# Routed attention and a gated feed-forward layer: mask products in tiles of 32 rows, and the work of three engines placed anew

## The chip, the cores and the metric

The kernel runs on one core of a Trainium2 chip. A core has TensorE (matrix products into PSUM), VectorE, ScalarE and GpSimd (work on whole tiles), and queues of DMAs, here mostly SyncE's. [...]semaphores tie the engines together. The metric is the device time of one execution in microseconds (us).

In the lines of the profile PE is TensorE, PEld its weight loads, DVE VectorE, ACT ScalarE, POOL GpSimd, SPq SyncE's DMA queue. A product's shape, such as 64*128, is rows by columns of the array that it uses. Every operation is recorded through one helper (line 63), so the tiles' names tell the groups apart.

## What is computed

```python
B, H, S, D = 4, 8, 768, 64 ; n_clusters = 16        # q, k, v: (B, H, S, D)
q_assign = argmax(einsum('bhsd,hcd->bhsc', q_n, c_n))   # q_n, k_n, c_n: unit length
k_assign = argmax(einsum('bhsd,hcd->bhsc', k_n, c_n))
mask = q_assign[:, :, :, None] == k_assign[:, :, None, :]
scores = where(mask, q @ k.T / sqrt(D), -1e9)
scores = scores - max(scores, axis=-1)
attn = exp(scores) ; attn = attn / (sum(attn, axis=-1) + 1e-9)
x = (attn @ v) as (B*S, H*D) = (3072, 512)
h = x @ w_in                                        # (3072, 2048)
out = (h * erf(softplus(h))) @ w_out                # (3072, 512)
```

All in float32 from outside. A query sees only the keys that fall to the same one of 16 centroids.

## The kernel before

**Two stages.** First the attention, for 16 pairs of heads (p = 0 to 15). Then the feed-forward layer in chunks of 512 tokens, its products by a scheme with seven products in place of eight, which needs sums of blocks ("forms", `left_forms` and `right_forms`, lines 518 and 527).

**A pair.** The two heads e = 0 and 1 of a pair lie on partitions 0 to 63 and 64 to 127 of transposed tiles qT and kT, so a product over D = 64 uses half of the array's rows, and those of the two heads go beside each other. A unit of work is 128 keys (j = 0 to 5) by one half of the queries (384), for both heads; a pair has 12 units. A *period* (`period(p, i)`, i = 0 to 5) handles two of them.

**What the mask is made of.** `choose` (VectorE: sims, the largest, hot, hotT) gives each token a one-hot row over the 16 centroids. `masks` multiplies it by the constant `pick` (64 rows) into PSUM, and ScalarE copies it to qm (0 or 1) or km (0 or -BIG, by `scale` and `bias=nbig`). qm and km have 64 rows a head: 16 for the centroids, and one (row SH = 32) that carries a shift in qm and 1 in km. The product km x qm added to q x k then gives the score less a shift where the centroids agree, and something hugely negative elsewhere.

**The shift** is a bound on the largest score, found one half ahead, by `maxima_step`: for 128 queries (t) and a half of the keys, TensorE multiplies bf16 copies qv, kv (call it v) and then adds qm x km (m) on the same PSUM tile `wide`; VectorE reduces the 768 columns to a maximum. Two steps make a period. After six of them a small reduce writes `lowest`, six products turn it (`turn`), and two copies (ScalarE, 1x384) put it into row SH of qm, before the scores of that half.

**Order of TensorE in a period**: turn (i = 0 and 3), v1 m1, `products` of both units (q x k, float32, into the two PSUM tiles sc), v2 m2, `scores` of both units (km x qm added: s and s'), similarities of the pair after the next (i = 3), `attend` of the two units before (128 keys by 64 columns), and at i = 0 and 3 the divide's products with `minus`. The four mask products of a pair stand in `MASKS` by period and place: place 0 ahead of `products`, 1 behind them, 2 behind the scores.

**The other engines.** ScalarE: exp of the two sc tiles (`curve`, into pr), the mask copies, the copies qv and kv, two steps (Ln, Exp) of the divide. VectorE: the reduces, transposes of the loaded q and k, `choose`, the rest of the divide. GpSimd: sums of pr over the keys (`accumulate`, into a part of more_out). All three also turn the feed-forward weights, loaded as 64-bit words, into float32, in small steps spread over the periods: `size_and_rest` and `sign` (ScalarE), `bounded` and `shifted` (VectorE), `summed` (GpSimd), for two of 22 pieces in a pair. The table `FORMS` says in which periods of pairs 11 to 15 VectorE computes the forms of w_in and of the first x.

**Order.** Most engines' instructions stay as the program writes them (`InOrder`). Later DMAs are issued on SyncE's queue where the framework places them. Buffers that matter: `wide` is single, sc double, pr eight deep, `turned[0]` and `turned[1]` are two PSUM banks which take turns for attend, divide, turn, similarities and the mask products.

Of the kernel before, what the change touches and what calls it, by code (L numbers as in the profile page):

```python
# [36 lines left out]

UP = 2.0**16
PLACES = 5
FORMS = {  # L40
    11: {5: 1}, 12: {0: 1, 2: 1, 5: 1}, 13: {0: 1, 2: 1, 5: 1}, 14: {0: 2, 2: 1, 3: 1, 5: 1},
    15: {0: 1, 2: 1, 3: 2, 4: 2, 5: 2},
}
BIG = 2.0**60
FLOOR = 2.0**50
EPS = 2.0**-70
SH = 2 * C
NPT = NJ + 2
N_LATE = 10
LAST_X = 11  # L50
MASKS = {(0, 1): ("k", 0), (2, 0): ("q", 0), (2, 2): ("k", 1), (5, 0): ("q", 1)}
FIRST_MASKS = {(2, 0): ("k", 0), (2, 1): ("q", 0), (2, 2): ("k", 1), (5, 0): ("q", 1)}


class InOrder:
# [16 lines left out]
def kernel(  # L72
# [157 lines left out]
    def fetch(n):  # L230
# [2 lines left out]
        words = t.rearrange("p (n w) -> p n w", w=2)  # L233
        steps[n] = words[:, :, 1], words[:, :, 0], t.bitcast(I16)[:, 1 : 4 * LC : 4]

    def size_and_rest(n):
        w, (hi, lo, _) = w_steps[n][0], steps[n]
        ae.activation(out=w, in_=hi, func=ACT.Abs, scale=UP)
        ae.activation(out=lo.bitcast(I32), in_=lo.bitcast(U32), func=ACT.Copy, scale=2.0**-29)

    def bounded(n):
        w = w_steps[n][0]
# [15 lines left out]

    ve.memset(nbig, 0.0)
    for e in range(2):  # L260
        ve.memset(nbig[e * D : e * D + C], -BIG)
        ve.memset(nbig[e * D + SH : e * D + SH + 1], 1.0)
    for t in maxima:
        ve.memset(t, FLOOR)
    ve.memset(pick, 0.0)
# [81 lines left out]
        if p < NPAIR:  # L347
            ae.copy(out=pairs[p][nm + "v"], in_=pairs[p][nm + "T"])

    def masks(p, nm, half, bank):  # L350

        if p >= NPAIR:
            return lambda: None
        st = pairs[p]
        cols = slice(half * HW, (half + 1) * HW)
        r = slice(0, D) if nm == "q" else slice(D, P)
        won = bank[:, 0:HW]
        te.matmul(won, lhsT=pick[r, half], rhs=st["hotT"][r], start=True, stop=True)
        if nm == "q":
            return lambda: ae.activation(out=st["qm"][:, cols], in_=won, func=ACT.Relu)  # L360
        return lambda: ae.activation(
            out=st["km"][:, cols], in_=won, func=ACT.Identity, bias=nbig, scale=BIG
        )

    turns = []

    def maxima_step(p, i, sm=wide):

        st = pairs[p]
        nmx = maxima[p % 2]  # L370
        t, half = divmod(i, 2)
        for a, b, start in (("qv", "kv", True), ("qm", "km", False)):
            for e in range(2):
                r = slice(e * D, (e + 1) * D)
                te.matmul(
                    sm[:, e, 0:HW], lhsT=st[a][r, t * P : (t + 1) * P],
                    rhs=st[b][r, half * HW : (half + 1) * HW], start=start, stop=not start,
                )
        ve.tensor_reduce(
            out=nmx[:, :, t, half], in_=sm[:, :, 0:HW], axis=AX.X, op=ALU.max, negate=True  # L380
        )
        if i in (NJ - 1, 2 * NJ - 1):
            h = i // NJ
            ve.tensor_reduce(
                out=lowest[h][:, :, SH::D].rearrange("p t e -> p e t"),
                in_=nmx[:, :, h * HJ : (h + 1) * HJ], axis=AX.X, op=ALU.min,
            )
            turns.append((p, h))

    def turn(p, h, copies=(ae.copy, ae.copy)):  # L390

        st = pairs[p]
        pn = turned[h][:, 0:HW].rearrange("p (t n) -> p t n", t=HJ)
        for t in range(HJ):
            for e in range(2):
                cols = slice(e * D, (e + 1) * D)
                te.matmul(pn[cols, t], lhsT=lowest[h][:, t, cols], rhs=identb, start=True, stop=True)
        for e, copy in zip(range(2), copies):
            r = slice(e * D + SH, e * D + SH + 1)
            copy(out=st["qm"][r, h * HW : (h + 1) * HW], in_=pn[r].rearrange("p t n -> p (t n)"))  # L400
        st["shift", h] = True

# [20 lines left out]
    def scores(u):  # L423

        p, half, j = units[u]
        st = pairs[p]
        sc = sc_of[u]
        assert ("shift", half) in st
        for e in range(2):
            r = slice(e * D, (e + 1) * D)  # L430
            te.matmul(
                sc[:, e, 0:HW], lhsT=st["km"][r, j * P : (j + 1) * P],
                rhs=st["qm"][r, half * HW : (half + 1) * HW], start=False, stop=True,
            )
# [226 lines left out]
        sums_of[n, s, lot] = gsp.tile([P, 3, FG, P], F32, name="g_more")  # L661
        return left_forms(ve, *g_parts(n, s, lot))

    def rest(n):
        return [lambda: None] * n

    def gates(n, lot, which=(0, 1), between=()):
        work = list(between)
        for s in which:
            curves, products_of = gate(n, lot, s)  # L670
            if s == which[0]:
                work = [curves] + work + rest(7 - len(work)) + products_of
            else:
                work += [curves, *sums, *rest(3)] + products_of
            sums = add_hidden(n, lot, s)
        return work + sums

# [27 lines left out]
    def run(work):  # L705
        for _ in work:
            pass

    def step_ahead(u):
        p, i = divmod(u + NJ, 2 * NJ)
        if p < NPAIR:
            maxima_step(p, i)

    forms = sum((left_forms(ve, *w_in_parts(f, 2)) for f in range(0, HF, 2)), [])
    routing = [iter(())]
    part = [iter(())]

    def period(p, i):  # L720
# [4 lines left out]
        def mask(place):  # L725
            which = (MASKS if p else FIRST_MASKS).get((i, place))
            if which:
                return masks(p + 1, *which, turned[0 if i in (0, 5) else 1])
            return lambda: None

        if u > 0:
# [3 lines left out]
            step_ahead(u)  # L735
        mask(0)()
        next(part[0], None)
        if u == 2:
            next(routing[0])
        products(u)  # L740
        products(u + 1)
        mask(1)()
        if u > 0:
            step_ahead(u + 1)
        next(part[0], None)
        scores(u)
        scores(u + 1)
        later = mask(2)
        if i == 3:
            similarities(p + 2)  # L750
            routing[0] = choose(p + 2)
        curve(u)
        later()
        curve(u + 1)
        if u == 0:
# [5 lines left out]
            vectors(1, "q")  # L761
            vectors(1, "k")
        if i == 0 and early(n1 - 1):
            shifted(n1 - 1)
            sign(n1 - 1)
        elif i == 1 and early(n1):
            size_and_rest(n1)
        elif i == 2 and early(n1):
            bounded(n1)
        elif i == 3 and early(n1):  # L770
            shifted(n1)
            sign(n1)
        elif i == 4 and early(n2):
            size_and_rest(n2)
        elif i == 5 and early(n2):
            bounded(n2)
        for work in forms[: FORMS.get(p, {}).get(i, 0)]:
            work()
            forms.remove(work)
        if i == 3:  # L780
            for _ in range(3):
                next(routing[0], None)
        if i == 0:
            if p:
                transposes(p + 2, "q")
        elif i == 1:
            load(p + 1, "v", v, vp)
            if p == 0:
                run(routing[0])
                transposes(2, "q")  # L790
        elif i == 2:
            transposes(p + 2, "k")
        elif i == 4:
            vectors(p + 2, "k")
        elif i == 5:
            run(routing[0])
            vectors(p + 2, "q")
        if u > 0:
            for w in (u - 2, u - 1):
                accumulate(w)  # L800
            if i == 1 and early(n1 - 1):
                summed(n1 - 1)
            elif i == 4 and early(n1):
                summed(n1)
            for w in (u - 2, u - 1):
                attend(w)
            if i % HJ == 0:
                part[0] = divide(u - 1)
                next(part[0])
        mask(3)()  # L810


# [23 lines left out]
    for r in (0, D):  # L836
        for half in range(2):
            for e in range(2):
                c = r + half * Q + e * C
                ve.tensor_copy(  # L840
                    out=pick[r : r + D, half, e * D : e * D + C], in_=first[r : r + D, c : c + C]
                )
    also = ps_s.tile([P, 2, 512], F32, name="sc", tag="s")
    products(0)
# [11 lines left out]
    for n in range(PLACES - 1):  # L856
        fetch(n)
    for i in range(NJ):
        maxima_step(0, i, also if i % 2 else wide)
        if i == 1:  # L860
            masks(0, "q", 1, turned[1])()
        if i < NJ - 1:
            warm(2, turned[0], zeros)
# [7 lines left out]
    for p in range(NPAIR):  # L871
# [3 lines left out]
            load_x(0)  # L875
            load_x(1)
        if p == LAST_X + 2:
            forms += right_forms(ve, *x_parts(0))
    for work in forms:
        work()  # L880
    u = len(units)
    for w in (u - 2, u - 1):
# [46 lines left out]
    aside_work += all_weights(0, 4) + out_forms[0] + out_forms[1]  # L929
    hidden(0, 0, {0: finish_attention})  # L930
    finish_aside()
    aside_work += together(rest(2) + gates(0, 0, (0,)), all_weights(4, N_LATE))
    hidden(0, 1, pace=2, first=ve.tensor_copy)
    finish_aside()
    for n in range(NCHUNK):
# [5 lines left out]
        project(n, 0, 2 if n else 3)  # L941
        finish_aside()
        if n == 0:
            aside_work += together(gates(0, 1, (1,)), rest(2) + [fence] + out_forms[2] + out_forms[3])
            hidden(1, 0, first=ve.tensor_copy)
        elif n + 1 < NCHUNK:
            hidden(n + 1, 0)
# [41 lines left out]
```

## Time and profile before

| | us |
|---|---|
| median of 3 runs | 1015.81 (1015.75 to 1015.94) |
| the profiled execution | 1015.54 |
| its span, first to last instruction | 1013.8 |
| attention: start to the last attend product | 0 to 429.4 |
| feed-forward layer | 429.3 to 1013.8 |
| one pair of heads in the steady part (p = 1 to 10) | 25.83 |
| mean granted TensorE clock | 1.000 |

The costliest operations of the attention, from the groups by shape (mean of one):

| engine, operation | count | ns |
|---|---|---|
| TensorE km,qm or kv,qv, 64*128, 384 columns bf16 | 756 | 322, 328 |
| TensorE q x k, 64*128, 384 columns float32 | 768 | 484, 482 |
| TensorE attend, 128*64, 386 columns float32 | 768 | 500 |
| VectorE reduce for the maxima | 189 | 956 |
| ScalarE exp | 192 | 810 |
| GpSimd add of pr | 160 | 1750, 1847 |
| VectorE transpose of 768 columns | 30 | 963 to 972 |
| ScalarE mask copies km, qm | 63 | 578, 494 |
| ScalarE size, rest, sign of a weight piece | | 679, 682, 1368 |
| VectorE bounded, shifted of a weight piece | | 417, 417 |

The length of one product [...]is longer than the distance between two starts. That is why distances of starts are used for TensorE.

### The profile page before, as it was taken

To read this page: it belongs to the slowest core of one execution; us is meant where nothing else is said; L and a number is where in the kernel's file an instruction comes from. 1 tells how busy PE (TensorE), PEld (TensorE's weight loads), DVE (VectorE), ACT (ScalarE), POOL (GpSimd) and SP (SyncE) were. 2 spreads that over 40 slices of the span, in tenths; PEclk is the share of its full clock that TensorE was granted. 3 is DMA by queue.
4 is the path that set the end of the run, shared out by engine and by line. 5 is a ranking of instruction groups with operands and counts; after the bars stand their busy time and mean duration, and the time that the engine had idled before them with its cause. 6 is when DMAs were issued, how large, how long until landed. Compare 5 with 4: busy or idle time off the path is not lost.

```text
span 1013.8 us, 15440 instructions
## 1 busy us (share of the span) xinstructions
PE 1006.4 (99%) x5930; PEld 724.0 (71%) x5930; DVE 695.5 (69%) x1305; ACT 513.5 (51%) x673; POOL 346.5 (34%) x229
## 2 busy tenths in 40 slices
PE   8999999999999999999999999999999999999998
PEld 3555555555555555488888888888888888888887
DVE  8777777777777777879766564756565647565753
ACT  3788888888887666467714232222324150505050
POOL 1777777777777667844030000000000000000000
PEclk9999999999999999999999999999999999999999
DMA  9344444444344311052000100110001000000001
GB/s 218 67 103 100 99 103 104 105 105 105 83 105 104 63 32 33 16 174 68 17 1 33 51 1 1 42 42 1 18 24 42 1 22 22 1 1 21 21 1 41
DMA packets 141641, 55.55 MB, mean 55 GB/s; under 512 B 127104, under 2 KB 131456, under 8 KB 141568
## 3 DMA queue, kind: packets, MB, share of 16 engines
q1 hardware_dynamic: 139216, 54.28, 20.9%
q8 instruction: 46, 0.75, 0.3%
q10 hardware_dynamic: 2352, 0.30, 0.2%
q14 instruction: 27, 0.22, 0.1%
HBM read 41.98 MB, written 12.58 MB: 54 GB/s over the span
## 4 chain that ended last, share of the span: by engine, by line
PE 97%; DVE 1%; DMA 1%; POOL 0%; ACT 0%; SPq 0%; issue 0%; DVEq 0%; ACTq 0%; POOLq 0%
PE bank L63 43%; PE turned L63 32%; PE sc L63 15%; PE wide L63 7%; DVE nmx L63 1%; POOL more_out L63 0%; DMA in_k<-in_k_dram 0%; DMA in_q<-in_q_dram 0%; DVE kT L63 0%; SPq L63 0%; DVE sims L63 0%; ACT inv L63 0%; DVE qT L63 0%; ACT pr L63 0%; DVE den L63 0%
## 5 line engine op out<-in xcount | busy, mean ns | idle before, releaser
L63 POOL TENSOR_TENSOR more_out<-more_out,pr 128x768 f32<-128x768 f32 x128 | 224.0, 1750 | 68.0 <-ACT pr L63 62.9
L63 DVE TENSOR_REDUCE nmx<-wide 128x2 f32<-128x768 f32 x189 | 180.7, 956 | 88.6 <-PE wide L63 64.3
L63 ACT ACTIVATE pr<-sc 128x768 f32<-128x768 f32 x192 | 147.1, 810 | 78.1 <-PE sc L63 78.1
L63 PE MATMUL turned<-pr,in_v 128*64 128x386 f32 x768 | 145.4, 500 | 0.1
L63 DVE TENSOR_TENSOR g<-bank,g 128x256 f32<-128x256 f32 x222 | 89.5, 421 | 53.2 <-PE bank L63 46.7
L63 PE MATMUL bank<-x_own,w_in 128*128 128x256 f32 x424 | 104.5, 380 | 0.0
L63 PE MATMUL bank<-w_out,g 128*128 128x256 f32 x448 | 103.1, 379 | 0.0
L63 PE MATMUL sc<-qT,kT 64*128 64x384 f32 x528 | 99.7, 484 | 0.0
L63 PEld LDWEIGHTS turned<-pr,in_v 128*64 128x64 f32 x768 | 46.6, 136 | 69.8 <-issue 65.1
L63 PEld LDWEIGHTS bank<-w_out,g 128*128 128x128 f32 x448 | 85.1, 190 | 11.6
L63 PEld LDWEIGHTS bank<-x_own,w_in 128*128 128x128 f32 x424 | 80.3, 190 | 12.2 <-issue 1.2
L63 ACT COPY g<-bank 128x256 f32<-128x256 f32 x28 | 10.4, 372 | 152.2 <-PE bank L63 148.2
L63 DVE TENSOR_TENSOR osb<-bank,osb 128x256 f32<-128x256 f32 x87 | 35.4, 419 | 72.8 <-ACT osb L63 25.4
L63 ACT ACT_TABLE_LOAD x48 | 61.6, 1283 | 45.9 <-DVE g L63 40.9
L63 POOL TENSOR_TENSOR more_out<-pr,pr 128x768 f32<-128x768 f32 x32 | 59.1, 1847 | 50.0 <-ACT pr L63 38.5
L63 PE MATMUL bank<-x_more,more_in 128*128 128x256 f32 x296 | 76.0, 379 | 0.0
L63 PEld LDWEIGHTS <-qv 64*128 64x128 bf16 x384 | 25.6, 93 | 65.2 <-issue 51.0
L63 PE MATMUL wide<-kv,qv 64*128 64x384 bf16 x378 | 69.4, 328 | 1.1 <-ACT km L63 0.6
L63 PE MATMUL wide<-km,qm 64*128 64x384 bf16 x378 | 68.3, 322 | 0.0
L63 PEld LDWEIGHTS sc<-qT,kT 64*128 64x128 f32 x528 | 56.2, 187 | 16.6 <-issue 1.2
L63 PE MATMUL bank<-more_out,g_more 128*128 128x256 f32 x272 | 64.3, 379 | 0.0
L63 DVE TENSOR_TENSOR g<-a_s,g 128x512 f32<-128x512 f32 x96 | 62.4, 687 | 1.4 <-ACT a_s L63 1.4
(162 smaller groups left out, 1704.8 us busy)
## 6 DMA issues: line engine op xcount, KB each, us to landing
x_own<-in_moe_w_in_dram SPq DMA_DIRECT2D x13, 512.0 KB, 4.0
in_v<-in_v_dram SPq DMA_DIRECT2D x32, 192.0 KB, 2.9
x_dram<-more_out SPq DMA_DIRECT2D x32, 192.0 KB, 2.2
x_own<-x_dram SPq DMA_DIRECT2D x6, 1024.0 KB, 5.1
out_dram<-osb SPq DMA_DIRECT2D x23, 256.0 KB, 2.0
in_k<-in_k_dram SPq DMA_DIRECT2D x59, 96.0 KB, 2.6
in_q<-in_q_dram SPq DMA_DIRECT2D x58, 96.0 KB, 3.1
g_more<-in_moe_w_out_dram SPq DMA_DIRECT2D x6, 512.0 KB, 3.4
```

Of the source, the lines that this page charges most:

```text
L63: ins = getattr(self.engine, name)(*args, **kw)
```

## The change

- Within the 64 rows a head, qm and km are laid out anew. The shift's row is now row 0; the centroids stand in rows 1 to 16, and once more in rows 33 to 48. `pick` writes both copies. In km the second copy has 0 in its own shift row. So rows 0 to 31 alone make a mask with shift, and rows 32 to 63 alone a mask without.
- `scores` multiplies only rows 0 to 31 of each head. The second maxima step of a period takes its mask passes (m2) from rows 32 to 63, and they are issued behind the first `scores`. v2, m1 and the passes of other steps keep 64 rows. TensorE's order is v1 m1, products, v2, s, m2, s'.
- Mask products of place 2 use 32 rows (`narrow`); k's first half moves from place 1 of period 0 to place 2 there, q's second half from place 0 of period 5 to place 2. The copy of km for k's first half is VectorE's.
- Work of VectorE and ScalarE stands in other periods: hotT in period 0 between the two reduces, the q transpose in period 5 (of the pair three ahead), both bf16 copies in period 4, `bounded` and `shifted` in periods 0 and 3, `size` at the end of period 3 and `rest` in period 5. `choose` puts its maxima beside an sc tile, not beside `wide`. GpSimd takes `summed` ahead of its adds.
- Of the 20 forms, up to eight are GpSimd's, two in each of pairs 12 to 15; VectorE's stand in pairs 12 to 15.
- The remaining lines rename `rest` to `idle` and add memsets for `nbig`.

```diff
-FORMS = {
-    11: {5: 1}, 12: {0: 1, 2: 1, 5: 1}, 13: {0: 1, 2: 1, 5: 1}, 14: {0: 2, 2: 1, 3: 1, 5: 1},
-    15: {0: 1, 2: 1, 3: 2, 4: 2, 5: 2},
-}
+FORMS = {12: {0: 1}, 13: {0: 1}, 14: {0: 1, 3: 1}, 15: {0: 1, 3: 2, 4: 2, 5: 2}}
+POOL_FORMS = range(12, 16)
-SH = 2 * C
-MASKS = {(0, 1): ("k", 0), (2, 0): ("q", 0), (2, 2): ("k", 1), (5, 0): ("q", 1)}
+MASKS = {(0, 2): ("k", 0), (2, 0): ("q", 0), (2, 2): ("k", 1), (5, 2): ("q", 1)}
...
-        ve.memset(nbig[e * D : e * D + C], -BIG)
-        ve.memset(nbig[e * D + SH : e * D + SH + 1], 1.0)
+        for n in range(2):
+            r = e * D + n * Q
+            ve.memset(nbig[r : r + C + 1], -BIG)
+            ve.memset(nbig[r : r + 1], 1.0 - n)
...
-    def masks(p, nm, half, bank):
+    def masks(p, nm, half, bank, narrow=False, copied_by=ae):
...
+        if narrow:
+            r = slice(r.start + half * Q, r.start + (half + 1) * Q)
         won = bank[:, 0:HW]
         te.matmul(won, lhsT=pick[r, half], rhs=st["hotT"][r], start=True, stop=True)
...
+        if copied_by is ve:
+            return lambda: ve.tensor_scalar(
+                out=st["km"][:, cols], in0=won, scalar1=BIG, scalar2=nbig, op0=ALU.mult, op1=ALU.add
+            )
...
-    def maxima_step(p, i, sm=wide):
+    def maxima_step(p, i, sm=wide, behind=False):
...
+        passes("qv", "kv", True, slice(0, D))
+        if behind:
+            yield
+        passes("qm", "km", False, slice(Q, D) if behind else slice(0, D))
...
@@ scores @@
             r = slice(e * D, (e + 1) * D)
+            r = slice(r.start, r.start + Q)
...
@@ period @@
+        if i == 0 and p:
+            run(routing[0])
...
-        if u > 0:
-            step_ahead(u + 1)
+        second = step_ahead(u + 1, True) if u > 0 else iter(())
+        next(second, None)
+        scores(u)
+        next(second, None)
         next(part[0], None)
-        scores(u)
         scores(u + 1)
         later = mask(2)
         if i == 3:
             similarities(p + 2)
-            routing[0] = choose(p + 2)
+            routing[0] = choose(p + 2, sc_of[u + 1][:, 0])
...
         if i == 0 and early(n1 - 1):
+            bounded(n1 - 1)
             shifted(n1 - 1)
             sign(n1 - 1)
...
-        elif i == 2 and early(n1):
+        elif i == 3 and early(n1):
             bounded(n1)
-        elif i == 3 and early(n1):
-            shifted(n1)
             sign(n1)
-        elif i == 4 and early(n2):
-            size_and_rest(n2)
         elif i == 5 and early(n2):
-            bounded(n2)
+            rest(n2)
...
-        if i == 0:
-            if p:
-                transposes(p + 2, "q")
...
         elif i == 4:
             vectors(p + 2, "k")
+            vectors(p + 2, "q")
         elif i == 5:
-            run(routing[0])
-            vectors(p + 2, "q")
+            transposes(p + 3, "q")
...
+            for w in (u - 2, u - 1):
+                accumulate(w)
+            if i % HJ == 1 and p in POOL_FORMS and forms:
+                forms.pop(0)[1]()
...
+        if i == 3 and early(n2):
+            size(n2)
```

More of the change, by code (lines that the diff above doesn't have):

```diff
@@ L50 @@
 LAST_X = 11
-MASKS = {(0, 1): ("k", 0), (2, 0): ("q", 0), (2, 2): ("k", 1), (5, 0): ("q", 1)}
-FIRST_MASKS = {(2, 0): ("k", 0), (2, 1): ("q", 0), (2, 2): ("k", 1), (5, 0): ("q", 1)}
+MASKS = {(0, 2): ("k", 0), (2, 0): ("q", 0), (2, 2): ("k", 1), (5, 2): ("q", 1)}
+FIRST_MASKS = {(2, 0): ("k", 0), (2, 1): ("q", 0), (2, 2): ("k", 1), (5, 2): ("q", 1)}
 class InOrder:
@@ L234, in fetch, with size, rest @@
         steps[n] = words[:, :, 1], words[:, :, 0], t.bitcast(I16)[:, 1 : 4 * LC : 4]
+    def size(n):
+        ae.activation(out=w_steps[n][0], in_=steps[n][0], func=ACT.Abs, scale=UP)
+    def rest(n):
+        lo = steps[n][1]
+        ae.activation(out=lo.bitcast(I32), in_=lo.bitcast(U32), func=ACT.Copy, scale=2.0**-29)
     def size_and_rest(n):
-        w, (hi, lo, _) = w_steps[n][0], steps[n]
-        ae.activation(out=w, in_=hi, func=ACT.Abs, scale=UP)
-        ae.activation(out=lo.bitcast(I32), in_=lo.bitcast(U32), func=ACT.Copy, scale=2.0**-29)
+        size(n)
+        rest(n)
     def bounded(n):
@@ L371, in maxima_step, with passes @@
         t, half = divmod(i, 2)
-        for a, b, start in (("qv", "kv", True), ("qm", "km", False)):
+        def passes(a, b, start, rows):
             for e in range(2):
-                r = slice(e * D, (e + 1) * D)
+                r = slice(e * D + rows.start, e * D + rows.stop)
                 te.matmul(
@@ L384, in maxima_step @@
             ve.tensor_reduce(
-                out=lowest[h][:, :, SH::D].rearrange("p t e -> p e t"),
+                out=lowest[h][:, :, ::D].rearrange("p t e -> p e t"),
                 in_=nmx[:, :, h * HJ : (h + 1) * HJ], axis=AX.X, op=ALU.min,
@@ L398, in turn @@
         for e, copy in zip(range(2), copies):
-            r = slice(e * D + SH, e * D + SH + 1)
+            r = slice(e * D, e * D + 1)
             copy(out=st["qm"][r, h * HW : (h + 1) * HW], in_=pn[r].rearrange("p t n -> p (t n)"))
@@ L662, in add_hidden, with idle @@
         return left_forms(ve, *g_parts(n, s, lot))
-    def rest(n):
+    def idle(n):
         return [lambda: None] * n
@@ L671, in gates @@
             if s == which[0]:
-                work = [curves] + work + rest(7 - len(work)) + products_of
+                work = [curves] + work + idle(7 - len(work)) + products_of
             else:
-                work += [curves, *sums, *rest(3)] + products_of
+                work += [curves, *sums, *idle(3)] + products_of
             sums = add_hidden(n, lot, s)
@@ L707, in run, with step_ahead @@
             pass
-    def step_ahead(u):
+    def step_ahead(u, behind=False):
         p, i = divmod(u + NJ, 2 * NJ)
-        if p < NPAIR:
-            maxima_step(p, i)
-    forms = sum((left_forms(ve, *w_in_parts(f, 2)) for f in range(0, HF, 2)), [])
+        steps = maxima_step(p, i, behind=behind) if p < NPAIR else iter(())
+        if not behind:
+            run(steps)
+        return steps
+    forms = []
+    for f in range(0, HF, 2):
+        forms += zip(*(left_forms(e, *w_in_parts(f, 2)) for e in (ve, ge)))
     routing = [iter(())]
@@ L727, in mask @@
             if which:
-                return masks(p + 1, *which, turned[0 if i in (0, 5) else 1])
+                return masks(p + 1, *which, turned[0 if i in (0, 5) else 1], place > 1, ve if i == 0 else ae)
             return lambda: None
@@ L767, in period @@
             size_and_rest(n1)
-        elif i == 2 and early(n1):
+        elif i == 3 and early(n1):
             bounded(n1)
-        elif i == 3 and early(n1):
-            shifted(n1)
             sign(n1)
-        elif i == 4 and early(n2):
-            size_and_rest(n2)
         elif i == 5 and early(n2):
-            bounded(n2)
-        for work in forms[: FORMS.get(p, {}).get(i, 0)]:
-            work()
-            forms.remove(work)
+            rest(n2)
+        for _ in range(min(len(forms), FORMS.get(p, {}).get(i, 0))):
+            forms.pop(0)[0]()
         if i == 3:
-            for _ in range(3):
+            next(routing[0], None)
+            if early(n1):
+                shifted(n1)
+            for _ in range(2):
                 next(routing[0], None)
-        if i == 0:
-            if p:
-                transposes(p + 2, "q")
         elif i == 1:
@@ L794, in period @@
             vectors(p + 2, "k")
+            vectors(p + 2, "q")
         elif i == 5:
-            run(routing[0])
-            vectors(p + 2, "q")
+            transposes(p + 3, "q")
         if u > 0:
-            for w in (u - 2, u - 1):
-                accumulate(w)
             if i == 1 and early(n1 - 1):
@@ L840 @@
                 ve.tensor_copy(
-                    out=pick[r : r + D, half, e * D : e * D + C], in_=first[r : r + D, c : c + C]
+                    out=pick[r : r + D, half, e * D : (e + 1) * D].rearrange("p (n c) -> p n c", n=2)[:, :, 1 : C + 1],
+                    in_=first[r : r + D, c : c + C].unsqueeze(1).to_broadcast([D, 2, C]),
                 )
@@ L858 @@
     for i in range(NJ):
-        maxima_step(0, i, also if i % 2 else wide)
+        run(maxima_step(0, i, also if i % 2 else wide))
         if i == 1:
@@ L877 @@
         if p == LAST_X + 2:
-            forms += right_forms(ve, *x_parts(0))
-    for work in forms:
+            forms += zip(*(right_forms(e, *x_parts(0)) for e in (ve, ge)))
+    for work, _ in forms:
         work()
@@ L931 @@
     finish_aside()
-    aside_work += together(rest(2) + gates(0, 0, (0,)), all_weights(4, N_LATE))
+    aside_work += together(idle(2) + gates(0, 0, (0,)), all_weights(4, N_LATE))
     hidden(0, 1, pace=2, first=ve.tensor_copy)
@@ L943 @@
         if n == 0:
-            aside_work += together(gates(0, 1, (1,)), rest(2) + [fence] + out_forms[2] + out_forms[3])
+            aside_work += together(gates(0, 1, (1,)), idle(2) + [fence] + out_forms[2] + out_forms[3])
             hidden(1, 0, first=ve.tensor_copy)
```

## The prediction

> **What bounds the kernel now.** I read the page first (span, share of each engine, slices, chain), then TensorE's own timeline inside one attention period, then the windows of one whole pair of heads.
>
> ```profile
> span 1013.8 us, 15440 instructions
> PE 1006.4 (99%) x5930; PEld 724.0 (71%) x5930; DVE 695.5 (69%) x1305; ACT 513.5 (51%) x673; POOL 346.5 (34%) x229
> ...
> PE   8999999999999999999999999999999999999998
> ...
> PE 97%; DVE 1%; DMA 1%; POOL 0%; ACT 0%; SPq 0%; issue 0%; DVEq 0%; ACTq 0%; POOLq 0%
> ```
>
> TensorE is busy in every slice and carries 97% of the chain. "Busy" alone doesn't say that it streams without holes, so here are the starts of its instructions in the period i = 1 of one pair (start, length, then the pieces merged):
>
> ```profile
> 280.77 0.34 PE L63 MATMUL wide<-kv,qv 64*128 64x384 bf16 x2
> 280.95 0.33 PE L63 MATMUL wide<-km,qm 64*128 64x384 bf16 x2
> 281.11 1.45 PE L63 MATMUL sc<-qT,kT 64*128 64x384 f32 x8
> 282.40 0.33 PE L63 MATMUL wide<-kv,qv 64*128 64x384 bf16 x2
> 282.56 0.33 PE L63 MATMUL wide<-km,qm 64*128 64x384 bf16 x2
> 282.73 0.49 PE L63 MATMUL sc<-qm,km 64*128 64x384 bf16 x4
> 283.14 1.52 PE L63 MATMUL turned<-pr,in_v 128*64 128x386 f32 x8
> 284.59 0.34 PE L63 MATMUL wide<-kv,qv 64*128 64x384 bf16 x2
> ```
>
> Two 64-row products of 384 columns in bf16 lie side by side, and such a pair holds TensorE 0.16 us (282.40, 282.56, 282.73). So the period (3.82 us) is a list of slots without a wait. Where the tile shape changes there is a hole. The last pair of sc starts one slot after 282.73, at 282.89, and the attend products (128x64) start 0.25 later, 0.09 more than a slot. Back from 128x64 the next period starts 1.45 after 283.14, where four slots of 0.32 would be 1.28; the rest is about 0.10 of hole and 0.05 of a first slot whose weights couldn't be loaded ahead. Its bf16 counterpart costs 0.01 (280.77 to 280.95 is 0.17 where 0.16 is usual). A change of columns or of rows alone pays too:
>
> ```profile
> 265.30 0.85 PE L63 MATMUL turned<-more_out,ccT 128*32 128x384 f32 x8
> 266.08 1.19 PE L63 MATMUL turned<-pr,in_v 128*64 128x386 f32 x6
> ```
>
> ```profile
> 13.17 0.32 PE L63 MATMUL turned<-hotT,pick 64*128 64x384 bf16 x1
> 13.43 0.50 PE L63 MATMUL turned<-lowest,identb 128*128 128x384 bf16 x2
> ```
>
> The first goes from 128x32 to 128x64: two slots of 0.33 and 0.32, then 0.78 until 266.08, a hole of 0.1. The second goes from 64 to 128 rows: 0.26 where a slot is 0.16. Over the pair 258.76 to 284.59 the other engines have room:
>
> ```profile
> 258.76:284.59 25.83, 25.83 (x202) 13.16 (x201) 19.86 (x31) 20.90 (x34) 19.96 (x13) 1.00 0.39 86
> ```
>
> Columns after the length: TensorE, weight loads, VectorE 19.86, ScalarE 20.90, GpSimd 19.96 of 25.83 us. The six periods last 4.17, 5.25, 3.82, 4.15, 4.64, 3.82 (i = 2, 3, 4, 5, 0, 1), the same in every pair.
>
> **What the Trainium skill says.** "TensorEngine Tiling (Array Packing)", section Tiling Modes: a change of tiling mode, not of tile, drains the engine, and tiles otherwise run independently. The trace agrees, with the holes of 0.09 to 0.10 above. "TensorE: Matmul & The Clock Gate", Part 3, Measured speedup: four 32-row tiles at 512 columns ran 3.07 times as fast. No 32-row tile is in this trace. Its section on LDWEIGHTS says that a load's time follows the columns, not the rows; the 64x128 bf16 load takes 0.093 us here, and I take the same for 32x128. "SBUF — State Buffer", SBUF: two separate sides: GpSimd and a VectorE operation with two SBUF inputs exclude each other for a whole instruction. The trace agrees: the same form takes 0.68 beside an idle GpSimd and 2.17 beside an adding one:
>
> ```profile
> 416.21 0.68 DVE L63 TENSOR_TENSOR more_in<-more_in,w_in 128x512 f32<-128x512 f32 x1
> 416.81 2.17 DVE L63 TENSOR_TENSOR w_in<-w_in 128x512 f32<-128x512 f32 x1
> ```
>
> **The change part by part.** I write v for the kv,qv passes, m for the km,qm mask passes of a maxima step (1 and 2 in a period), s and s' for the mask products of scores.
>
> *Four row groups at once.* Before: v2, m2, s, s' in four slots, 0.74 us from v2 to attend. After: v2; a change to 32-row tiles; s (rows 0-31, 64-95) and m2 (rows 32-63, 96-127) in one slot; s'; the change to attend. That is 0.16 + 0.09, then 0.17 (weights not ahead), then 0.16 + 0.09: about 0.68. Saved: 0.06 a period, since 0.10 of the slot goes back to the new change of shape. This cost isn't in the trace for 64 to 32 rows. Bounds: nothing (tiles of the same columns might not drain), 0.16 (the slot itself); I take 0.10, as all four kinds of change seen pay it.
>
> *Mask of q's second half* moves in period 5 from a 64-row product ahead of the scores to a 32-row one (rows 32-63) beside s' (rows 0-31, 64-95). It cost 0.16 there (2.53 from v1 to attend, against 2.37 in period 1) and now nothing. *k's first half* (period 0) goes behind s' on a row group that s' uses: 0.16 before, 0.16 after; a ragged 0.01 is saved. *Period 2* keeps its 64-row mask (0.16); the narrow one was balanced by it already. Sum per pair: 6 x 0.06 + 0.16 + 0.01 = 0.54 with the unrounded starts.
>
> Pairs 1 to 14: 14 x 0.54 = 7.55. Pair 0: five periods and the mask 0.46, less two extra changes of shape in its first period (64 to 32 and back, 0.20): 0.26. Pair 15: three periods save 0.19, three have no maxima left and pay the change for nothing, 0.31: minus 0.12.
>
> *Who must keep up.* Same work, shorter periods (25.3 us), so each wait is placed by durations.
> - ScalarE: leaves to VectorE one km copy (0.58); total 20.9 less 0.6 = 20.3 of 25.3. Tight spot: period 5 now ends with pr, qm, pr, rest (0.70, 0.4 to 0.5, 0.70, 0.69 from 2.32 on), then the two shift copies (0.95), which end 5.74 to 5.85 after the period's start; s of period 0 is due at 5.82. Cost 0 to 0.1 a pair for 10 pairs; I take 0.
> - VectorE: hotT (0.57) fits between the two reduces of period 0 (1.41 to 1.98; the second starts at 2.27). The new km copy (0.56 by the prologue's qm row) ends at 3.70, and the divide's product into the same bank comes at 3.82. Before, a bank was freed 0.06 ahead (km in period 2) without a hole. Behind km wait bounded and shifted (0.42 each), done before the next reduce at 5.1. I take 0, bound 0.15 x 14.
> - GpSimd: summed goes ahead of the adds; its last add before a divide still ends over 1 us early in my layout. Queued DMAs: q's load follows the transpose from period 0 to period 5 on SP's queue, ahead of v's load, with about 13 us until use; hidden.
>
> *Forms.* Eight of twenty leave VectorE for GpSimd in pairs 12 to 15, where no weight sums are left; 1.3 us each in gaps of 0.8 to 2. The holes of 0.08 in period 3 of pairs 12 to 14 (5.33 against 5.25) go: minus 0.24. In the tail VectorE has one form more after period 3 (seven for six, 2.1 us each beside GpSimd), so the form b12 is ready at 432.7 on the old clock and piece 7 wants it at 432.03: plus 0.65, less 0.3 from a shorter wait for GpSimd at 420.57. Bounds minus 0.3 to plus 2; I take 0.35.
>
> *Prologue.* Four more memsets (0.09 each) and wider pick copies: the warm-up starts 0.37 later, nearly all behind the q transpose; 0.10.
>
> The MoE stage (430 to 1014) has the same instructions: 0.
>
> Sum: 7.55 + 0.26 - 0.12 + 0.24 - 0.35 - 0.10 = 7.5 us. Span 1006.3; the profiled execution took 1015.54, so 1008.1 for it; the median lies 0.27 above: **1008.3 us**.
>
> **The rivals.**
> 1. *The change of shape is free* when only rows are split: 97 changes (84 in pairs 1 to 14, 13 in pairs 0 and 15) x 0.10 more: 998.3. For: rows 64 and 32 share the 128 columns. Against: 64 to 128 rows pays 0.10 at 13.43.
> 2. *New waits eat a part.* The shift copies and the km copy each late by 0.1 to 0.2 a pair, with a slow tail: 3 to 6 us back, 1011 to 1015. For: margins of 0.05 to 0.12 us. Against: equal margins hold today.
> 3. *Slower: four row groups don't stream together.* The trace never has more than two products of 128 columns at once; the four of the 128x32 shape write 32 partitions each. If s and m2 go one after the other, 0.16 comes back each period and the new change stays: 0.10 worse instead of 0.06 better, 92 x 0.16 = 14.7 more: about 1023. It decides as soon as the shared slot takes more than 0.17 + 0.06 + 0.16/6 = 0.26 us. Against: the skill's 3.07, and the pairs of today.
> 4. *It hides nothing because TensorE isn't the bound*: excluded by the list of slots without waits.
>
> **How the numbers follow.** Forecast 0.64 (own range 1006 to 1011), rival 1 0.10, rival 2 0.15, rival 3 0.11. The range is 1000 to 1014: it leaves out rival 3, most of rival 1 and the end of rival 2. 0.2% is 2.0 us, about what a measurement tells from no change. Faster: 0.64 + 0.10 + 0.08 = 0.82; the rest of rival 2 and a little of 3 make 0.08 the same; 0.10 slower.
>
> **What would show it.** Right: from v2 to the attend products 0.68 in period 1, s and m2 starting together 0.25 after v2, periods of about 3.76 (i = 1, 4), 3.93 (5), 4.57 (0), 5.19 (3), 25.3 a pair; VectorE forms still at 2.1 in the tail. Rival 1: m2 at 0.16 after v2. Rival 2: holes before s in period 0, released by ScalarE's qm, or before the divide's products, by VectorE's km. Rival 3: starts of s and m2 0.16 apart. If the MoE stage changes its length, or the gain isn't spread evenly over the pairs, I am wrong about where it comes from.

## The result and the profile after

| | before | changed |
|---|---|---|
| median of 6 runs | 1015.82 | 1011.59 (1011.19 to 1012.82) |
| ratio to before | | 0.996, 95% interval 0.9947 to 0.9973 |
| span of the profiled execution | 1013.8 | 1009.3 |
| one pair in the steady part | 25.83 | 25.50 |

The changed kernel is faster by 4.2 us, where 7.5 were forecast. Its page:

```profile
span 1009.3 us, 15518 instructions
PE 1001.3 (99%) x5930; PEld 699.8 (69%) x5930; DVE 699.8 (69%) x1315; ACT 501.6 (50%) x659; POOL 349.2 (35%) x237
...
PE   8999999999999999999999999999999999999998
...
PE 96%; DVE 2%; DMA 1%; SPq 0%; issue 0%; ACT 0%; DVEq 0%; ACTq 0%
```

TensorE is still the bound, but VectorE has gone from 1% to 2% of the chain. One percent of the span is 10 us, so this is a rounded hint of a few microseconds. TensorE's own timeline in a period 1 (start, length, pieces merged) shows the core of the change (the helper stands in line 60 of this kernel, so L60):

```profile
252.28 0.34 PE L60 MATMUL wide<-kv,qv 64*128 64x384 bf16 x2
252.45 0.33 PE L60 MATMUL wide<-km,qm 64*128 64x384 bf16 x2
252.62 1.45 PE L60 MATMUL sc<-qT,kT 64*128 64x384 f32 x8
253.91 0.33 PE L60 MATMUL wide<-kv,qv 64*128 64x384 bf16 x2
254.16 0.34 PE L60 MATMUL sc<-qm,km 32*128 32x384 bf16 x2
254.17 0.33 PE L60 MATMUL wide<-km,qm 32*128 32x384 bf16 x2
254.34 0.33 PE L60 MATMUL sc<-qm,km 32*128 32x384 bf16 x2
254.59 1.52 PE L60 MATMUL turned<-pr,in_v 128*64 128x386 f32 x8
256.04 0.34 PE L60 MATMUL wide<-kv,qv 64*128 64x384 bf16 x2
```

s and m2 start 0.01 apart and share one slot (s' follows 0.17 later): four row groups of 32 stream together. They start 0.25 after v2, 0.09 more than a slot, so 64 to 32 rows is a change of shape that is paid for. From v2 to attend there are 0.68 us where there were 0.74, and the period is 3.76 where it was 3.82.

All periods came as forecast but one. In the order i = 2, 3, 4, 5, 0, 1 they last 4.10, 5.19, 3.76, 3.93, **4.76**, 3.76. Period 0 was forecast at 4.57 and had been 4.64. Here it is, in the timeline of all engines around the divide of one pair:

```profile
249.41 0.34 PE L60 MATMUL wide<-km,qm 32*128 32x384 bf16 x2
...
249.74 0.32 PE L60 MATMUL turned<-hotT,pick 32*128 32x384 bf16 x1
249.85 0.96 DVE L60 TENSOR_REDUCE nmx<-wide 128x2 f32<-128x768 f32 x1 [0.34 <-PE wide L60]
...
249.99 1.52 PE L60 MATMUL turned<-pr,in_v 128*64 128x386 f32 x8
250.72 0.61 DVE L60 TENSOR_SCALAR km<-turned,nbig 128x384 bf16<-128x384 f32 x1
251.25 0.88 DVE L60 TENSOR_SCALAR w_out<-w_out 128x512 f32<-128x512 f32 x2
...
251.48 0.87 PE L60 MATMUL turned<-more_out,minus 128*64 128x384 f32 x4
```

The mask product of k's first half is there at 250.06 (249.74 + 0.32), but VectorE's copy of it stands behind the reduce and ends at 251.33. The divide's products use the same bank. The last attend slot starts 0.97 after 249.99 plus the 0.05 of a first slot, so they could follow at 251.34 (0.32 later); they start at 251.48. Their first slot then also lacks its weights (0.05). Together 0.19 a pair, without a line in the table of waits: the profile books the hole as none of TensorE's idle time, because the modelled lengths of the products before it (249.99 + 1.52 = 251.51) run past it. Distances of starts show it.

The spans account for the rest. From period 2 of pair 0 to that of pair 14: 362.09 before, 357.53 after, minus 4.56. From there to the first product of the feed-forward layer: minus 0.86. The prologue: plus 0.18. The first block of the feed-forward layer: plus 0.76, with one wait on a form (`DVE x_own`):

```profile
425.93 1.03 PE L60 MATMUL bank<-x_more,more_in 128*128 128x256 f32 x4
427.45 1.13 PE L60 MATMUL bank<-x_own,w_in 128*128 128x256 f32 x4 [0.50 <-DVE x_own L60]
```

From the divide in that block to the end there are 578.2 us in both. The sum is minus 4.5.

### The profile page after: what moved, and what is told of

It reads as the page before. It is cut to its first block, busy times and chain, and to the rows that moved or that the text cites. A ratio compares the mean times of both kernels' runs of the same rounds, so it can differ in the third digit from the quotient of the medians.

```text
span 1009.3 us, 15518 instructions
## 1 busy us (share of the span) xinstructions
PE 1001.3 (99%) x5930; PEld 699.8 (69%) x5930; DVE 699.8 (69%) x1315; ACT 501.6 (50%) x659; POOL 349.2 (35%) x237
## 4 chain that ended last, share of the span: by engine, by line
PE 96%; DVE 2%; DMA 1%; SPq 0%; issue 0%; ACT 0%; DVEq 0%; ACTq 0%
PE bank L60 43%; PE turned L60 32%; PE sc L60 16%; PE wide L60 5%; DVE nmx L60 1%; DMA in_k<-in_k_dram 0%; SPq L60 0%; DMA in_q<-in_q_dram 0%; DVE x_own L60 0%; DVE more_in L60 0%; DVE x_more L60 0%; DVE w_in L60 0%; DVE kT L60 0%; DVE turned L60 0%; DVE sims L60 0%
## 5 line engine op out<-in xcount | busy, mean ns | idle before, releaser
L60 DVE TENSOR_REDUCE nmx<-wide 128x2 f32<-128x768 f32 x189 | 180.9, 957 | 80.7 <-PE wide L60 80.0
L60 POOL TENSOR_TENSOR more_out<-more_out,pr 128x768 f32<-128x768 f32 x128 | 216.4, 1691 | 28.7 <-ACT pr L60 22.8
L60 ACT ACTIVATE pr<-sc 128x768 f32<-128x768 f32 x192 | 148.8, 811 | 91.0 <-PE wide L60 86.6
L60 PE MATMUL turned<-pr,in_v 128*64 128x386 f32 x768 | 145.4, 500 | 0.0
L60 DVE TENSOR_TENSOR g<-bank,g 128x256 f32<-128x256 f32 x222 | 89.7, 422 | 53.1 <-PE bank L60 46.5
L60 PE MATMUL bank<-x_own,w_in 128*128 128x256 f32 x424 | 104.6, 380 | 0.5 <-DVE x_own L60 0.5
L60 PE MATMUL bank<-w_out,g 128*128 128x256 f32 x448 | 103.1, 379 | 0.0
L60 PE MATMUL sc<-qT,kT 64*128 64x384 f32 x528 | 98.2, 484 | 0.0
L60 PEld LDWEIGHTS turned<-pr,in_v 128*64 128x64 f32 x768 | 46.6, 136 | 69.9 <-issue 59.3
L60 PEld LDWEIGHTS bank<-w_out,g 128*128 128x128 f32 x448 | 85.1, 190 | 11.6
L60 PEld LDWEIGHTS bank<-x_own,w_in 128*128 128x128 f32 x424 | 80.3, 190 | 12.9 <-DVE x_own L60 0.9
L60 ACT COPY g<-bank 128x256 f32<-128x256 f32 x28 | 10.4, 372 | 152.4 <-PE bank L60 148.4
L60 DVE TENSOR_TENSOR osb<-bank,osb 128x256 f32<-128x256 f32 x87 | 35.5, 421 | 72.8 <-ACT osb L60 25.4
L60 PE MATMUL bank<-x_more,more_in 128*128 128x256 f32 x296 | 76.0, 379 | 0.0
L60 PEld LDWEIGHTS <-qv 64*128 64x128 bf16 x384 | 26.8, 93 | 68.5 <-issue 52.5
L60 POOL TENSOR_TENSOR more_out<-pr,pr 128x768 f32<-128x768 f32 x32 | 59.3, 1854 | 28.4 <-ACT pr L60 28.4
L60 PEld LDWEIGHTS sc<-qT,kT 64*128 64x128 f32 x528 | 52.4, 187 | 19.9 <-ACT pr L60 1.2
L60 PE MATMUL wide<-kv,qv 64*128 64x384 bf16 x378 | 64.8, 328 | 1.1 <-ACT km L60 0.6
L60 PE MATMUL bank<-more_out,g_more 128*128 128x256 f32 x272 | 64.3, 379 | 0.0
L60 DVE TENSOR_TENSOR g<-a_s,g 128x512 f32<-128x512 f32 x96 | 62.5, 689 | 1.4 <-ACT a_s L60 1.4
L60 PE MATMUL wide<-km,qm 64*128 64x384 bf16 (+1 forms) x378 | 62.5, 327 | 0.0
```

The lines of the kernel that those rows point to most:

```text
L60: ins = getattr(self.engine, name)(*args, **kw)
```

## The experiments

Spans are compared with the changed kernel's 1009.3. Where a time is of one run alone, the text says so.

### Are the tiles the gain, or the new layout?

All mask products at 64 rows, everything else as changed:

```diff
-            r = slice(r.start, r.start + Q)
...
-        passes("qm", "km", False, slice(Q, D) if behind else slice(0, D))
+        passes("qm", "km", False, slice(0, D))
...
-turned[0 if i in (0, 5) else 1], place > 1, ve if i == 0 else ae)
+turned[0 if i in (0, 5) else 1], False, ve if i == 0 else ae)
```

> Change: scores, m2 and all mask products use 64 rows again, in the changed kernel's order and with its layout of work. Theory A (the gain is four row groups in one slot, less one change of shape): 0.06 us more in each period with maxima and 0.16 more in period 5, about 26.0 us a pair against 25.50, the span about 7 us above the changed kernel's, 1016 to 1017, so above the kernel before. Rival (the gain comes from the work laid out anew on the other engines): the span stays within 1.5 us of 1009.3.

Span 1015.3, 1017.68 us in one run; periods 4.15, 5.25, 3.82, 4.15, 4.75, 3.82 (i = 2, 3, 4, 5, 0, 1), together 25.92. Theory A holds: 0.06 in a plain period, 0.06 + 0.16 in period 5, 6.0 us in all. That is 1 us less than it said, since period 0 doesn't grow: it stays at 4.75, about 0.1 over the 4.64 of the kernel before, so the hole behind km is there too, a little smaller. Without its tiles the new layout is slower than the kernel before, by 1.5 us of span, which is about what this hole costs in 14 pairs. TensorE's timeline of one period 2 has the four products at 64 rows one after the other, 0.16 apart (a line's 0.48 covers the products of the two heads, which start 0.16 apart in this period):

```profile
183.64 0.48 PE L60 MATMUL wide<-kv,qv 64*128 64x384 bf16 x2
183.80 0.48 PE L60 MATMUL sc<-qm,km 64*128 64x384 bf16 x2
183.97 0.48 PE L60 MATMUL wide<-km,qm 64*128 64x384 bf16 x2
184.13 0.48 PE L60 MATMUL sc<-qm,km 64*128 64x384 bf16 x2
```

### What does the change of shape cost by itself?

m2 in front at 64 rows, s and s' alone at 32:

```diff
-        second = step_ahead(u + 1, True) if u > 0 else iter(())
+        second = iter(())
+        if u > 0:
+            step_ahead(u + 1)
```

> Change: m2 goes back in front of the scores and to 64 rows; s and s' keep 32 rows, so the change of shape is paid and nothing lies beside it. Theory A (any change of the tile's rows costs 0.10, whatever follows): from v2 to attend 0.83 instead of 0.68, period 1 at about 3.91, a pair about 26.4, the span about 13 us above the changed kernel's. Rival (the 0.10 is the price of four weight loads and four products starting at once, not of the change of shape): v2 to attend about 0.74, period 1 at 3.82, the span about 5 us above.

Span 1021.6, 1023.31 us in one run; period 1 is 3.92, a pair 26.28. Theory A holds, and its rival, which put the span 5 us above the changed kernel's, falls: it is 12.3 above. TensorE's timeline:

```profile
182.21 0.33 PE L60 MATMUL wide<-km,qm 64*128 64x384 bf16 x2
182.47 0.50 PE L60 MATMUL sc<-qm,km 32*128 32x384 bf16 x4
182.90 1.52 PE L60 MATMUL turned<-pr,in_v 128*64 128x386 f32 x8
```

s starts 0.26 after m2 though only two tiles follow, not four. The 0.10 belongs to the change of rows. A plain period is 0.10 longer than with 64 rows throughout (3.92 against 3.82), and 0.16 longer than with m2 in the slot of s (3.76). So of the 0.16 that sharing brings, the change of shape takes 0.10.

### Who makes the hole in period 0?

The copy of km back on ScalarE:

```diff
-turned[0 if i in (0, 5) else 1], place > 1, ve if i == 0 else ae)
+turned[0 if i in (0, 5) else 1], place > 1, ae)
```

> Change: the copy of km for k's first half (period 0) goes back from VectorE to ScalarE, all else as in the changed kernel. Theory A (the 0.14 us hole before the divide's products in period 0 comes from VectorE's km copy, which is queued behind the second reduce and frees the bank late): the hole goes and period 0 falls from 4.76 to about 4.57; but ScalarE's queue of period 0 grows by 0.58, its Exp of the divide ends about 1.95 us into period 1, and the attend products of period 1 wait some 0.2 for VectorE's den: period 1 from 3.76 to about 3.95, so that a pair stays near 25.5. Theory B (the hole is GpSimd's last add, or the weight load of the divide's products): period 0 stays at 4.76 whoever copies.

Span 1010.0, 1011.77 us in one run. Period 0 is 4.57: the hole is VectorE's. Period 1 is 3.96 in pairs with weight steps, 3.76 from pair 12 on, where ScalarE has none left; period 2 grows from 4.10 to 4.17 in the former (to 4.47 in pair 1). ScalarE and the two that hang on it, in the timeline of one period 1 (which begins at 150.81):

```profile
151.52 0.60 ACT L60 ACTIVATE inv<-turned,alleps 128x384 f32<-128x384 f32 x1
...
152.15 0.52 ACT L60 ACTIVATE inv<-inv 128x384 f32<-128x384 f32 x1
...
152.70 0.56 DVE L60 SCALAR_TENSOR_TENSOR den<-turned,inv 128x384 f32<-128x384 f32 x1 [0.40 <-ACT inv L60]
...
153.32 1.52 PE L60 MATMUL turned<-pr,in_v 128*64 128x386 f32 x8
```

The Exp ends at 152.67, VectorE waits 0.40 for it, and attend, which writes the bank that den reads, starts 2.51 into the period where it could at 2.31. A wait was traded for one of the same size, on another bank. Here TensorE starts 0.06 after VectorE's end (152.70 + 0.56), and at the divide of the changed kernel 0.15 after it; why the two differ is not shown. The divide's products also wait for GpSimd's sum, and TensorE's queue has an instruction that only waits in between (251.38 to 251.43).

### km ahead of the reduce

The second reduce of period 0 is held back until VectorE has copied km:

```diff
         passes("qm", "km", False, slice(Q, D) if behind else slice(0, D))
+        if behind:
+            yield
...
         next(second, None)
+        if i:
+            run(second)
         next(part[0], None)
         scores(u + 1)
         later = mask(2)
+        if not i:
+            later()
+            later = lambda: None
+            run(second)
```

> Change: in period 0 VectorE copies km before the second reduce, not behind it. Theory A: the bank is free 0.5 us before the divide's products; period 0 falls from 4.76 to about 4.57, a pair from 25.50 to 25.31, the span by 14 x 0.19 = 2.7 us to about 1006.7, the time to about 1008.9. The reduce ends 0.5 later, still 0.3 us before wide is wanted again. Theory B (GpSimd's add or the weight load makes the hole): period 0 stays at 4.76 and the time at 1011.6.

1011.87 us, ratio 0.9965 (0.9952 to 0.9979), span 1009.9. Period 0 is 4.57 in pairs 1 to 14 but one, as theory A said, and still nothing was won: period 1 is 4.81 in pairs 12 to 14 (the next expectation counts them one too low), where VectorE computes a form in period 0. The timeline of one of them:

```profile
325.45 0.95 DVE L60 TENSOR_REDUCE nmx<-wide 128x2 f32<-128x768 f32 x1
...
326.20 1.82 POOL L60 TENSOR_TENSOR more_out<-pr,pr 128x768 f32<-128x768 f32 x1 [1.16 <-ACT pr L60]
...
326.31 2.26 DVE L60 TENSOR_TENSOR more_in<-w_in 128x512 f32<-128x512 f32 x1
...
328.49 0.95 DVE L60 TENSOR_REDUCE nmx<-wide 128x2 f32<-128x768 f32 x1
...
329.49 0.34 PE L60 MATMUL wide<-kv,qv 64*128 64x384 bf16 x2 [0.87 <-DVE nmx L60]
```

The reduce now ends later, so the form starts 0.11 behind GpSimd's add and takes 2.26 us. In the changed kernel the same form started 0.21 ahead of that add (328.14):

```profile
327.93 0.68 DVE L60 TENSOR_TENSOR more_in<-w_in 128x512 f32<-128x512 f32 x1
```

The next reduce is late, and with it v2: three times 1.05 us, 3.1 together, against the 14 x 0.19 = 2.7 that were won; the rest of the difference is a prologue 0.14 later. The expectation had placed the reduce and forgotten the form behind it.

### The repaired kernel

As above up to pair 11; from pair 12 on ScalarE, which is free there, copies km; and the forms of the first x stand ahead of the last four of w_in, which are wanted only in the second half of the hidden products:

```diff
...
+        if i or p > LAST_X:
+            run(second)
...
+        if not i and p <= LAST_X:
+            later()
+            later = lambda: None
+            run(second)
...
-turned[0 if i in (0, 5) else 1], place > 1, ve if i == 0 else ae)
+turned[0 if i in (0, 5) else 1], place > 1, ve if i == 0 and p <= LAST_X else ae)
...
-            forms += zip(*(right_forms(e, *x_parts(0)) for e in (ve, ge)))
+            forms[-4:-4] = zip(*(right_forms(e, *x_parts(0)) for e in (ve, ge)))
```

> Change, from the changed kernel: in pairs up to 11 VectorE copies km ahead of the second reduce of period 0; from pair 12 on, where ScalarE has no weight steps left, ScalarE copies it; and the four forms of the first x are put ahead of the last four of w_in, so that none of them is late for the first block of the feed-forward layer. Theory (the forecast missed by the 0.19 a pair at the divide, and km first failed in pairs 11 to 13 only because the form behind it met GpSimd's add): 25.31 in every pair, no 4.8 in period 1, no wait for x_own at the first block; the span 2.7 + 0.65 below the changed kernel's, about 1006.0, the time about 1008.3. Rival (something else fills the room, such as ScalarE's shift copies or the last forms): the span stays above 1007.5.

**1007.84 us** (1007.58 to 1008.75), ratio 0.9927 (0.9915 to 0.9939), span 1005.6. The changed kernel beside it on the same chip:

> The changed kernel itself, beside the repaired one on one chip. Span 1009.3 to 1009.7, time about 1011.6; the repaired one 3.3 us faster by the theory, the same by its rival.

It took 1011.13 us (1010.88 to 1011.29), span 1009.0. The repaired one is 3.3 us faster, and 7.6 faster than before (1015.46 there). The theory holds: all full pairs (1 to 13) but one last 25.31, and the products of the first block follow each other at 0.86 without a wait. Its order around the divide, to be read against the same stretch of the changed kernel above:

```profile
247.96 0.32 PE L60 MATMUL turned<-hotT,pick 32*128 32x384 bf16 x1
...
248.39 0.62 DVE L60 TENSOR_SCALAR km<-turned,nbig 128x384 bf16<-128x384 f32 x1 [0.67 <-PE turned L60]
248.92 0.95 DVE L60 TENSOR_REDUCE nmx<-wide 128x2 f32<-128x768 f32 x1
...
249.55 0.81 PE L60 MATMUL turned<-more_out,minus 128*64 128x384 f32 x4
```

km is done at 249.01, half a microsecond ahead of the divide's products.

### All forms on VectorE

> Change, from the changed kernel: all 20 forms are VectorE's again, in the periods of the kernel before. Theory A (the part of the forms is worth little: it takes 0.08 a pair from pairs 12 to 14 and costs 0.3 to 0.65 at the first block): the span within 1 us of 1009.3, period 3 of pairs 12 and 13 at 5.27, no wait for x_own at 427. Rival (in the shorter periods VectorE's forms meet GpSimd's adds, at 2.1 instead of 0.68 us): several periods of pairs 12 to 15 grow by up to 1 us, the span 1.5 to 5 us above 1009.3.

Only the tables were changed: `FORMS` as before, `POOL_FORMS = ()`. Span 1019.5, 1021.25 us in one run: theory A, mine, is wrong. The rival has the right kind, but the cost is twice its upper end. Periods 0 and 3 of pairs 12 to 14, period 0 of pair 15 and period 1 of pair 14 grow by 0.9 to 1.75 us, and period 4 of pair 15 by 0.46. TensorE's waits, and the cause of one of them in VectorE's timeline (GpSimd's adds run from 323.29 to 327.06):

```profile
PE wide L63 <- DVE nmx L63: 9.9, 11, 1.6
```

```profile
323.31 0.18 DVE L63 TENSOR_REDUCE lowest<-nmx 128x6 bf16<-128x18 f32 x1
323.40 2.12 DVE L63 TENSOR_TENSOR more_in<-w_in 128x512 f32<-128x512 f32 x1
325.44 0.96 DVE L63 STREAM_TRANSPOSE more_out<-in_q 128x768 f32<-128x768 f32 x1
326.34 0.91 DVE L63 TENSOR_REDUCE nmx<-wide 128x2 f32<-128x768 f32 x1
```

In the kernel before, the same form ran 0.09 ahead of GpSimd's add (327.15):

```profile
327.06 0.68 DVE L63 TENSOR_TENSOR more_in<-w_in 128x512 f32<-128x512 f32 x1
```

Now it starts 0.11 behind it, and the q transpose, which has moved into this period, stands in front of the reduce as well. So the rest of the new layout doesn't stand with the old places of the forms: the new ones are worth 10 us in it, though the prediction counted them as 0.24 won and 0.35 lost. How much of that is GpSimd's share, and how much the other periods that VectorE's own forms got, isn't shown: no run has all 20 on VectorE in other periods.

## Why the prediction was right, and where it was off

The time, 1011.59, lies in the range of 1000 to 1014 and was forecast as faster; the gain was 4.2 where 7.5 were forecast. The number itself is not the forecast's: it stands above the 1006 to 1011 that had 0.64, at the lower end of the 1011 to 1015 that rival 2 had with 0.15. The tiles came as worked out; that the total still lay in the range is owed to its width. By its steps:

- **Four row groups in one slot, less a change of shape: right**, in mechanism and size. 0.06 in each period, a change of 0.10, v2 to attend 0.68. The run at 64 rows gives the worth of the tiles (6.0 us), that with the scores alone at 32 rows the price of the change. Rival 1 (the change is free) and rival 3 (four don't stream together) fall with the starts of s and m2. (Rival 1's 998.3 would be 998.6 by its own rounded figures, which changes nothing.)
- **The mask of q's second half: right**: period 5 went from 4.15 to 3.93.
- **"The new km copy (0.56 by the prologue's qm row) ends at 3.70, and the divide's product into the same bank comes at 3.82 ... I take 0, bound 0.15 x 14": this step failed.** It cost 0.19 x 14 = 2.7 us, which is most of the 3.0 that the span misses. Three terms were small by a little. The reduce started 2.33 into the period, not 2.27; the copy took 0.61, not 0.56; so it ended at 3.81. And between VectorE's end and TensorE's start lie 0.15 where I had let 0.06 pass for enough, after a case in which ScalarE copied and nothing was seen (its copy ended 0.05 ahead of the product). Late products also lose the weights loaded ahead, 0.05 that was not in the bound. Rival 2 had named this place and this size.
- **ScalarE's shift copies: right at 0.** Period 0 of the repaired kernel is 4.57 with weight steps and without.
- **Forms in pairs 12 to 14, minus 0.24: right in kind, one pair too many.** The holes went (period 3 is 5.19 in pairs 12 and 13 as in the others), but pair 14 had none: without similarities its period 3 lasted 4.46 before and lasts 4.41 now. So it was 0.17.
- **The tail**: the late form cost 0.76 (of which 0.50 as a wait) where 0.65 had been worked out, and the wait for GpSimd in period 3 of pair 15 went.
- **Why the forms had to leave VectorE I had not seen.** The prediction read the 0.68 at 416.21 as a form beside an idle GpSimd. GpSimd's add starts at 416.31, so the form was 0.10 ahead of an adding one. The lines above show what this margin is worth: 0.09 to 0.21 ahead of the add a form takes 0.68, 0.11 behind it 2.12 and 2.26.
- **The prologue, plus 0.10**: plus 0.18 in this execution, in which k's first DMA landed late (VectorE waits 0.31 for it); minus 0.09 in the profile of the second measurement. So it is not told from noise.
- **The MoE stage (the feed-forward layer), 0: right** behind its first block.

One hole of 0.17 in one pair (behind pair 9 in both profiles of the changed kernel, behind pair 6 or 9 in four of its six variants) has no cause in the profile: VectorE stood 0.35 before a q transpose and waited for nothing that is shown. The two variants without the hole have the same stop, where it delays nothing. In all of them it comes after the same number of VectorE's recorded instructions (447, those that only wait included), except in the variant with km on ScalarE, where it comes after 128 fewer. This points to a place in VectorE's program rather than to the data that it waits for. The hole was not in the forecast, and its cause stays open.

## What to carry to other kernels

Where a stage is a list of TensorE slots without holes, price tiles by slots saved less changes of shape, and gather the small tiles so that one change serves them all. In such a stage a copy that frees a PSUM bank needs a margin to its next user that includes the hand-over between the engines (0.15 us at the divide, 0.06 at den), so lay out the queue in front of the copy before counting it as hidden. And when VectorE's queue is shifted, look at what stands at its end: a two-input operation that slips behind a GpSimd add by 0.1 us cost 1.4 to 1.6 us more here.

## What the runs showed of the hardware that was not expected

- TensorE's table of waits can miss a wait: a hole of 0.14 us ahead of the divide's products, 14 times, appears in none of its rows, since the modelled lengths of products overlap it.
- The part of the time outside the span varied more than the span: in the six runs of the changed kernel spans of 1009.3 to 1009.7 went with times of 1011.19 to 1012.82.
- From the modelled end of four products that start together to VectorE's reduce lie 0.08 to 0.11 us (249.41 + 0.34 to 249.85 in the changed kernel); behind the last two of a 64-row pair it was about 0.04 before.
